# A fused attention and gated-FFN kernel: the first chunk's second product in row tiles, with its exchanged weights and two batches' loads moved to make that possible

## The chip, the cores and the metric

The kernel runs on one core of a Trainium2 chip. Times are device microseconds (us) of that core, as medians of several executions. A profile is one execution taken by the hardware profiler; its span is about 1.7 us shorter than the time of the same execution. The kernel before had the TensorE clock at full speed (granted clock 0.998 to 1.0).

## The reference

A causal attention with a forget gate (8 batches, 8 heads, 576 tokens, head size 64) whose output, as a matrix of 4608 tokens by 512, goes through a gated FFN with 1536 inner columns. Everything is given and returned in 32-bit floats.

```python
scores = (q @ k.T) / sqrt(64) + (cum[:, None] - cum[None, :])   # cum: cumulative log of f; causal mask
attn   = softmax(scores) @ v                                    # -> x, 4608 x 512
out    = (sigmoid(x @ w_gate) * (x @ w_val)) @ w_out            # 512 -> 1536 -> 512
```

## The kernel before

The FFN walks over nine chunks of 512 tokens. A chunk has 36 steps: 24 for the first product (x by w_gate and w_val), 12 for the second (by w_out). The attention of later batches is slipped in between these steps: score units (matmul, exp on ScalarE, causal mask on GpSimd) and, four heads at a time, an output *burst*, 120 small matmuls that make sums and values, after which VectorE scales x and SyncE exchanges the two halves of its partitions.

"Row tiles" means that in place of one matmul of 128 rows there are two of 64 rows, one on each half of the partitions. Such a pair took as long as one 128-row matmul: 10.36/48 = 0.216 us in the first profile (L495, 96 matmuls at 296.99 us), against 0.21 to 0.22 for L504. The first product and the second product of chunks 1 to 6 are in that form (`g2_twin`); chunks 0, 7 and 8 use full 128-row matmuls (`g2_full`). For the second half of its work the twin form, as written here, reads the operands with their partition halves exchanged: `gvx` (the activations, exchanged in each such chunk after column tiles 5, 9 and 11 of twelve) and `wox` (the output weights, exchanged once).

```python
    swap_bf = wox[:, NFT - 1, 0:128]
    xt = gvx[:, 0, :].rearrange("p (a d) -> p a d", d=64)
    # ...
    def cross_w2(x):                       # one piece of the exchanged weights, 2 tiles, 128 KB
        dst, src = ((LO, HI), (HI, LO))[x % 2]
        fs = slice(x // 2 * 2, x // 2 * 2 + 2)
        nc.sync.dma_start(wox[dst, fs, :], wo[src, fs, :])
    # ...
    TWIN = range(1, NTC - 2)

    def g1_end(c, ft):                     # end of one column tile of the first product
        # ... tanh on ScalarE, gate on VectorE -> gv[:, ft, :]
        if ft in (5, 9, 11) and c in TWIN:
            fs = slice({5: 0, 9: 6, 11: 10}[ft], ft + 1)
            nc.sync.dma_start(gvx[LO, fs, :], gv[HI, fs, 0:TCH // 2])
            nc.sync.dma_start(gvx[HI, fs, :], gv[LO, fs, TCH // 2:TCH])

    def g2_twin(c, y):
        x, qq, g = y // 6, y // 3 % 2, y % 3
        fb = 4 + 2 * qq
        n = TCH // 2
        for ft in range(4 * g, 4 * g + 4):
            for half, bk, o in ((LO, fb, 0), (HI, fb + 1, n)):
                if x == 0:
                    lhsT, rhs = gv[half, ft, o + qq * NP:o + (qq + 1) * NP], wo[half, ft, :]
                else:
                    lhsT, rhs = gvx[half, ft, qq * NP:(qq + 1) * NP], wox[half, ft, :]
                nc.tensor.matmul(ps[:, bk, :], lhsT, rhs, ...)
        # ... stores after the last piece

    def g2_full(c, x):
        tt, g = (x % 4, x // 4) if c == 0 else (x // 3, x % 3)
        for ft in range(4 * g, 4 * g + 4):
            nc.tensor.matmul(ps[:, 4 + tt, :], gv[:, ft, tt * NP:(tt + 1) * NP], wo[:, ft, :], ...)
    # ... the schedule: put(step, what)
    for x, w in enumerate((5, 9, 12)):
        put(w, lambda x=x: load_w2(x))
    for x, w in enumerate((18, 21, 22, 23)):            # queries and keys of batches 2 and 3
        put(w, lambda x=x: load_qk(2 + x // 2, x % 2, ((0, 4),)))
    for x in range(NFT):                                # exchanged weights, in chunk 1
        put(38 + 2 * x, lambda x=x: cross_w2(x))
```

The softmax here doesn't subtract the row's maximum and nothing guards it: scores larger than these inputs give would overflow.

## Time and profile before

| before | |
|---|---|
| time, median of 3 runs | 373.72 us (373.67 to 373.79) |
| span of the profiled run | 373.4 us, granted clock 0.998 |
| TensorE busy | 359.3 us, 96% of the span |
| first, second, third burst begin (a second profile of this kernel) | 45.79, 62.12, 87.01 us |

Two lines of the page matter for what follows: the DMA engines' busy share in 40 slices of the span (in tenths, 9.3 us a slice), which the prediction used only to ask when the exchanged data land, and the queue q8, of the kind "instruction", with packets, megabytes and its share of 16 engines' time, which it did not use.

```profile
DMA  8999999599988976789984996596313131011002
...
q8 instruction: 41, 0.67, 0.8%
```

In ten of the first eleven slices, about 100 us, the DMA engines are busy for 0.8 or more of the time. The second line looks negligible, 0.8%. I take it to be TensorE's own program, which the page does not say: 41 packets of 0.67/41 MB = 16 KB, for an engine with 5259 matmuls and 5264 weight loads in the trace, 10,523/41 = 257 a packet. From the first packet (15.23 us) to the last (358.47) the trace holds about 10,126 of them, 253 for each of 40 packets. So I estimate a packet at 256 instructions, a number that the places of the pauses bear out below.

### The profile page before, as it was taken

Reading aid. Unit: us, or ns where it says so; the run is one execution under the profiler, and the core shown is the slowest. Engines: PE = TensorE matmul, PEld = TensorE weight load, DVE = VectorE, ACT = ScalarE, POOL = GpSimd, SP = SyncE. Lnnn points to the kernel's source line nnn. Section 1 sums busy time; section 2 is a strip of 40 time slices with the busy share of each in tenths; the row PEclk is TensorE's granted clock in tenths of the full one; section 3 lists DMA queues with packets and bytes.
Section 4 is the critical chain, followed back from the end, with each engine's and each line's share of the span. In section 5 each row is a group of like instructions: output and inputs, shape, how many; then the busy total and the mean of one; then the engine's idle time right before and its main releaser. Section 6 shows DMA issues by size and latency. Waiting matters only on the chain.

```text
span 373.4 us, 12210 instructions
## 1 busy us (share of the span) xinstructions
PE 359.3 (96%) x5259; PEld 192.0 (51%) x5264; DVE 176.5 (47%) x382; ACT 195.7 (52%) x294; POOL 168.3 (45%) x265
## 2 busy tenths in 40 slices
PE   2889999999999999999999999999999999999996
PEld 1547545455555545454665566545456544444442
DVE  5775482557375555274708370737064703312320
ACT  5868754574736472848374727471747313323321
POOL 8896745064826663559665946460415000000000
PEclk9999999999999999999999999999999999999999
DMA  8999999599988976789984996596313131011002
GB/s 157 233 209 256 194 182 217 173 213 154 158 164 196 157 84 63 168 182 134 142 185 105 185 177 138 148 159 83 99 59 76 32 102 58 3 56 58 0 24 90
DMA packets 101350, 49.24 MB, mean 132 GB/s; under 512 B 72001, under 2 KB 94401, under 8 KB 101297
## 3 DMA queue, kind: packets, MB, share of 16 engines
q0 software_dynamic: 48704, 20.65, 44.0%
q1 hardware_dynamic: 52448, 27.68, 30.8%
q8 instruction: 41, 0.67, 0.8%
q10 hardware_dynamic: 144, 0.13, 0.1%
q14 instruction: 13, 0.10, 0.1%
HBM read 37.90 MB, written 9.44 MB: 127 GB/s over the span
## 4 chain that ended last, share of the span: by engine, by line
PE 94%; ACT 2%; DMA 1%; issue 1%; DVE 1%; POOL 0%; ACTq 0%; POOLq 0%
PE ps L455 51%; PE ps L495 17%; PE ps L352 8%; PE ps L504 8%; PE ps L241 6%; PE ps L195 2%; PE ps L300 1%; DMA qk_in<-in_k_dram 1%; ACT eC L246 1%; ACT eB L246 0%; ACT eA L246 0%; ACT kT L200 0%; PE ps L417 0%; DVE kT L200 0%; POOL qk_in L97 0%
## 5 line engine op out<-in xcount | busy, mean ns | idle before, releaser
L455 PE MATMUL ps<-xR,w 64*128 64x512 bf16 x1728 | 205.1, 376 | 0.2
L465 DVE SCALAR_TENSOR_TENSOR gv<-sg,ps 128x512 bf16<-128x512 bf16 x108 | 74.0, 686 | 152.2 <-ACT sg L464 149.0
L455 PEld LDWEIGHTS <-w 64*128 64x128 bf16 x1728 | 86.2, 94 | 84.0 <-issue 2.5
L464 ACT ACTIVATE sg<-ps 128x512 bf16<-128x512 f32 x108 | 64.5, 598 | 85.1 <-PE ps L455 83.9
L248 POOL TENSOR_SCALAR_AFFINE_SELECT eC<-eC 128x256 bf16<-128x256 bf16 x32 | 12.9, 404 | 94.4 <-ACT eC L246 94.4
L241 PE MATMUL ps<-qT,kT 64*128 64x320 bf16 (+6 forms) x416 | 47.0, 275 | 2.0 <-ACT kT L200 1.1
L246 ACT ACTIVATE eC<-ps 128x896 bf16<-128x896 f32 (+1 forms) x32 | 28.1, 878 | 20.7 <-PE ps L241 20.4
L257 POOL TENSOR_TENSOR vg<-vb,g_bf 128x640 bf16<-128x640 f32 x30 | 37.8, 1261 | 0.0
L482 ACT ACTIVATE ob<-ps 128x512 f32<-128x512 f32 x35 | 19.6, 596 | 32.2 <-PE ps L504 20.1
L495 PE MATMUL ps<-wox,gvx 64*128 64x512 bf16 x288 | 35.7, 376 | 0.0
L241 PEld LDWEIGHTS <-kT 64*128 64x128 bf16 x416 | 22.9, 96 | 24.0 <-issue 4.9
L246 ACT ACTIVATE eA<-ps 128x896 bf16<-128x896 f32 (+2 forms) x33 | 30.5, 926 | 9.0 <-PE ps L241 8.5
L495 PE MATMUL ps<-wo,gv 64*128 64x512 bf16 x288 | 34.4, 376 | 0.0
L246 ACT ACTIVATE eB<-ps 128x768 bf16<-128x768 f32 (+2 forms) x33 | 27.4, 832 | 10.0 <-PE ps L241 9.2
L504 PE MATMUL ps<-wo,gv 128*128 128x512 bf16 x140 | 32.1, 380 | 0.3 <-issue 0.2
L271 DVE TENSOR_TENSOR xR<-ps,R 128x64 bf16<-128x64 f32 (+2 forms) x68 | 26.2, 429 | 2.1
L108 POOL DMA_DIRECT2D vb<-in_v_dram x30 | 25.2, 849 | 0.2 <-issue 0.2
L263 DVE STREAM_TRANSPOSE R<-r 128x576 f32<-128x576 f32 (+1 forms) x32 | 24.6, 770 | 1.1
L495 PEld LDWEIGHTS <-gvx 64*128 64x128 bf16 x288 | 15.7, 94 | 13.0 <-issue 0.4
L495 PEld LDWEIGHTS <-gv 64*128 64x128 bf16 x288 | 15.3, 94 | 13.7 <-issue 0.5
L246 ACT ACTIVATE eD<-ps 128x640 bf16<-128x640 f32 x30 | 21.1, 702 | 2.0 <-PE ps L241 2.0
L504 PEld LDWEIGHTS <-gv 128*128 128x128 bf16 x144 | 13.4, 98 | 16.7 <-issue 1.4
(82 smaller groups left out, 325.9 us busy)
## 6 DMA issues: line engine op xcount, KB each, us to landing
out_dram<-ob SPq DMA_DIRECT2D x35, 256.0 KB, 2.2
vb<-in_v_dram POOLq DMA_DIRECT2D x20, 256.0 KB, 5.4
xR<-xR SPq DMA_DIRECT2D x20, 144.0 KB, 4.1
gvx<-gv SPq DMA_DIRECT2D x12, 192.0 KB, 4.8
vb<-in_v_dram SPq DMA_DIRECT2D x8, 256.0 KB, 7.3
k_rows<-in_k_dram POOLq DMA_DIRECT2D x16, 128.0 KB, 6.0
q_rows<-in_q_dram POOLq DMA_DIRECT2D x16, 128.0 KB, 5.6
qk_in<-in_q_dram POOLq DMA_DIRECT2D x7, 288.0 KB, 6.7
```

Of the source, the lines that this page charges most:

```text
L108: eng.dma_start(vbs[b % 2][0:n, t, h0:h1, :], rows)
L241: nc.tensor.matmul(ps[:, sc + h, c:c + i1 - i0], k_at(p, jt)[hp, :], qT[hp, i0:i1], start=True, stop=True)
L246: nc.scalar.activation(e[:, :, 0:w], ps[:, sc:sc + 2, 0:w], ACTF.Exp, scale=scale)
L257: (eng or nc.gpsimd).tensor_tensor(out=vg[:, :, :, 0:D], in0=vbs[b % 2][:, :, 2 * a:2 * a + 2, :], in1=g_bf[:, :, 2 * p:2 * p + 2].unsquee ...
L263: nc.vector.transpose(R.rearrange("p (n c) -> p n c", c=32), r.unsqueeze(2).to_broadcast([128, r.shape[1], 32]))
L271: nc.vector.tensor_tensor(out=xR[:, a, r0:r0 + n], in0=psf[:, o + i:o + i + n], in1=R[:, i:i + n], op=ALU.mult)
L352: nc.tensor.matmul(psf[32 * qd:32 * qd + 32, o + a:o + z], lhsT_of(jt, qd), e_of(u, qd)[:, c:c + z - a], start=(y == 0), stop=(y == len(to ...
L455: nc.tensor.matmul(ps[:, bk, :], w1[half, head, ft * NP:(ft + 1) * NP], xR[half, sl, t0:t0 + TCH], start=(first and x == 0), stop=(last an ...
L464: nc.scalar.activation(sg, ps[:, fb, :], ACTF.Tanh, scale=0.5)
L465: nc.vector.scalar_tensor_tensor(out=gv[:, ft, :], in0=sg, scalar=1.0, in1=ps[:, fb + 1, :], op0=ALU.add, op1=ALU.mult)
L495: nc.tensor.matmul(ps[:, bk, :], lhsT, rhs, start=(x == 0 and ft == 0), stop=(x == 1 and ft == NFT - 1))
L504: nc.tensor.matmul(ps[:, 4 + tt, :], gv[:, ft, tt * NP:(tt + 1) * NP], wo[:, ft, :], start=(ft == 0), stop=(ft == NFT - 1))
```

## The change

The intent: make the second product of chunk 0 a twin as well, so that TensorE no longer changes between the 128-row form and the 64-row form of the score units there (about 0.11 us a change, as the prediction reads it from 0.97 against 0.86 us in the trace). For that the exchanged weights are needed earlier, in chunk 0, and they are made in six large pieces instead of twelve small ones. To make room on the DMA queues, the queries and keys of batch 3 are loaded in chunk 1, and those of batch 2 one or two steps later in chunk 0. An interim value `xt` moves out of `gvx`, which chunk 0 now uses.

```diff
-    xt = gvx[:, 0, :].rearrange("p (a d) -> p a d", d=64)        # now in an output buffer
@@ cross_w2
-        fs = slice(x // 2 * 2, x // 2 * 2 + 2)
+        fs = slice(x // 2 * 4, x // 2 * 4 + 4)
@@ rest_values (rest_turn reads it again as st["xt"])
+        ob = osb.tile([128, DM], FP32, tag="ob", name="ob")
+        xt = st["xt"] = ob[:, 0:DM // 4].bitcast(BF16).rearrange("p (a d) -> p a d", d=64)
@@
-    TWIN = range(1, NTC - 2)
+    TWIN = range(0, NTC - 2)
@@ g2_full
-        tt, g = (x % 4, x // 4) if c == 0 else (x // 3, x % 3)
+        tt, g = divmod(x, 3)
@@ schedule
-    for x, w in enumerate((18, 21, 22, 23)):
+    for x, w in enumerate((20, 22, 50, 54)):
         put(w, lambda x=x: load_qk(2 + x // 2, x % 2, ((0, 4),)))
-    for x in range(NFT):
-        put(38 + 2 * x, lambda x=x: cross_w2(x))
+    for x in range(6):
+        put((19, 21, 23)[x // 2], lambda x=x: cross_w2(x))
```

More of the change, by code (lines that the diff above doesn't have):

```diff
@@ L430, in rest_turn @@
         slot_free(1)
+        xt = st["xt"]
         halves = ((LO, 3), (HI, 2))
```

## The prediction

> **What bounds the kernel now.** I read the page first. TensorE is busy 359.3 of 373.4 us at full clock and the chain that ended last is 94% TensorE, so only what TensorE itself does, or waits for, sets the time. In the chain in order of time I then looked at chunk 0's second product (steps 24 to 35, line L504, one 128-row matmul per weight tile) and at the same stage of later chunks (L495, two 64-row matmuls side by side). Columns are start, length, engine and line, count.
>
> ```profile
> PE 359.3 (96%) x5259; PEld 192.0 (51%) x5264; DVE 176.5 (47%) x382; ACT 195.7 (52%) x294; POOL 168.3 (45%) x265
> PE 94%; ACT 2%; DMA 1%; issue 1%; DVE 1%; POOL 0%; ACTq 0%; POOLq 0%
> ...
> 296.99 10.36 PE ps L495 x96
> ```
>
> The last line is a whole second product in row tiles without anything between: 96 matmuls, 48 pairs, 10.36/48 = 0.216 us a pair. A 128-row matmul of L504 also takes 0.216 us (5.13 us for 23 records of 24, the trace having lost one: 5.13/24 = 0.214). So row tiles make no matmul faster; what can be won lies in the changes between forms. For that I read the timeline of TensorE, where starts can be compared: first chunk 0's second product with its score units (L241), then score units of the same shapes inside a first product (L455, row tiles already).
>
> ```profile
> 57.17 1.04 PE L504 MATMUL ps<-wo,gv 128*128 128x512 bf16 x4
> 58.14 0.36 PE L241 MATMUL ps<-qT,kT 64*128 64x448 bf16 x2
> 58.43 1.04 PE L504 MATMUL ps<-wo,gv 128*128 128x512 bf16 x4
> 59.40 0.53 PE L241 MATMUL ps<-qT,kT 64*128 64x256 bf16 x8
> 59.87 1.04 PE L504 MATMUL ps<-wo,gv 128*128 128x512 bf16 x4
> ...
> 80.98 0.35 PE L241 MATMUL ps<-qT,kT 64*128 64x448 bf16 x2
> 81.17 1.03 PE L455 MATMUL ps<-xR,w 64*128 64x512 bf16 x8
> 82.03 0.36 PE L241 MATMUL ps<-qT,kT 64*128 64x256 bf16 x4
> 82.23 1.03 PE L455 MATMUL ps<-xR,w 64*128 64x512 bf16 x8
> ```
>
> A group of four L504 matmuls holds TensorE from 57.17 to 58.14, 0.97 us; eight L455 ones hold it 82.03-81.17 = 0.86. The 448-column unit holds it 0.29 beside L504 and 0.19 beside L455. So each change between the 128-row and the 64-row form costs about 0.11 us, in each direction.
>
> Last, the engines that feed the output burst (L352) in the middle of this stage, from the timelines of ScalarE and GpSimd:
>
> ```profile
> 61.31 0.71 ACT L246 ACTIVATE eD<-ps 128x640 bf16<-128x640 f32 x1
> ...
> 59.91 1.26 POOL L257 TENSOR_TENSOR vg<-vb,g_bf 128x640 bf16<-128x640 f32 x1
> 61.13 0.63 POOL L248 TENSOR_SCALAR_AFFINE_SELECT eA<-eA 128x512 bf16<-128x512 bf16 x1
> 61.72 0.28 POOL L248 TENSOR_SCALAR_AFFINE_SELECT eB<-eB 64x128 bf16<-64x128 bf16 x1
> 62.09 0.41 POOL L248 TENSOR_SCALAR_AFFINE_SELECT eD<-eD 128x256 bf16<-128x256 bf16 x1
> ...
> 62.47 0.37 PE L352 MATMUL ps<-eD,g_bf 128*32 128x256 bf16 x4
> ```
>
> The burst starts at 62.08, just as ScalarE is done with eD (61.31+0.71 = 62.02), and its eD matmuls stand at 62.47 with 0.37 us, where the first burst's take 0.28: they wait for the mask of eD on GpSimd (62.09+0.41 = 62.50). So at this place ScalarE, GpSimd and TensorE are level. That decides how much of the saving survives.
>
> [...] The trace shows their mean busy share over 0.9 in most of the first 65 us and 0.24 in 65 to 70 us, so I take it that what is added before 65 us competes with loads.
>
> **The change part by part.**
> (a) Second product of chunk 0: out go 48 full matmuls (48 x 0.216 = 10.37 us), in come 48 pairs (10.36). Nothing. Twice the weight loads, 94 ns each, two in 216 ns: hidden, as in the later chunks.
> (b) Changes of form. Score units stand at four places between the quads: four changes out of the 128-row form, 4 x 0.105 = 0.42 us, and four back (B+D 0.41 for 0.29; C 0.29 for 0.19; A+B 0.47 for 0.36; D 0.24 for 0.13) = 0.44. Into the burst: the last quad held 62.08-61.08 = 1.00, estimated 0.95 in row tiles: 0.05. Out of it: last L352 start 64.24 to first L504 64.62 is 0.38; in chunk 1 from 103.78 to the first L495 at 103.93 is 0.15: 0.23. Transposes (64x64) are another form in both versions: no difference. Sum 0.42+0.44+0.05+0.23 = 1.14 us of TensorE.
> (c) What the other engines let through. From the first score unit (0.1 earlier) ScalarE runs eB, eD, eC without a pause in the kernel before, so eC's exp ends at 59.36 for 59.46, and GpSimd then runs the mask of eC, the value scaling, the masks of eA, eB, without a pause: all only 0.1 earlier. The mask of eB ends at 61.90, and that of eD, which no longer waits for ScalarE (its last exp gains the 0.35 us pause before eA and ends near 61.6), runs from about 61.88 to 62.29. TensorE would be at the burst by about 61.5, waits for ScalarE's eD until about 61.65, and its eD matmuls for GpSimd until 62.3. Against 62.50 that saves 0.2, not the 0.9 that TensorE had gained by there. After the burst the 0.23 of (b) comes in full. Sum 0.2+0.23 = about 0.45 us.
> (d) Exchanged weights, 12 transfers of 128 KB in chunk 1 become 6 of 256 KB in chunk 0. In SyncE's order they stand behind earlier pieces: the first pair goes once the first third of the output weights has landed (issued 33.97, landing some 8 to 9 us: about 43), the second behind gv of tile 9 (51.0), the third behind the exchange of the first burst's x (54.5 to 55.8), so issued by 57.0, then the last gvx pair by 58.3. Such a piece of 128 KB landed in 3.5 to 6.1 us, a last gvx in about 4; estimated here: all landed by about 63. The crossed half starts after the burst, near 64, and needs the last third near 66. Some 2 us to spare.
> (e) Value loads of batch 2 now stand behind these, issued from 58.3 instead of 55.85; they took 8.56 us to issue, landed by 67.8, and are wanted by the scaling at 74.1: still hidden.
> (f) Queries and keys of batch 3: four transfers leave 47 to 57 us and go to steps 50 and 54 (about 84 to 91 us), wanted at step 67 (106.6); they landed in 6 to 7.2 us. GpSimd pays the same 0.65 us each, behind the masks that the burst of step 52 needs. Hidden both times; it does relieve the queue exactly where (d) loads it.
> (g) The interim copy xt moves from gvx to an output buffer, free at that time: no cost. Outputs of chunk 0 are evicted two at step 32 and two at step 35 instead of one in each; the second pair needs about 1.3 us on ScalarE, and its banks are wanted 0.41+0.97+0.41 = 1.8 us later: no wait.
>
> **The rivals.**
> 1. The whole 1.14 us comes through (time 372.6): if GpSimd's chain in front of the burst is looser than I read. For it: the profile marks only short waits there. Against it: the eD matmuls of 0.37 us.
> 2. Late data (374 to 375): the crossed half at step 30 or 32 waits for wox or gvx. For it: the DMA engines are over 0.9 busy up to 65 us, and one value load needed 4.2 us on SyncE; landings beyond 8 us occur. Against it: 2 us to spare and four competing loads gone. A variant is the second burst's x exchange, issued at 68.8, wanted by chunk 1's first tiles at about 72.9, landing in 3.7: almost no room, so a value load still in the queue then would cost half a microsecond.
> 3. Nothing at all (373.7): the pauses of TensorE called "issue" (0.43 us at 127.6, 0.30 at 254.3) stand at no place that the program explains; 96 more matmuls and loads shift them, and may cost or give 0.3 us.
>
> **Range and chances.** 373.72 - 0.45 = 373.27, written as 373.2 as rival 1 is likelier than 2. The range reaches from the full saving, 372.6, to 373.8, where a small wait eats it. 2% is 7.5 us, more than the whole stage's overhead: faster 0.005, same 0.985, slower 0.01.
>
> **What would show it.** Right: no L504 in chunk 0, quads of 0.86 us from start to start, score units of 0.13 to 0.29; from the first second-product matmul (54.93) to the first transpose of step 36 about 14.3 us instead of 14.75; a wait of TensorE for ScalarE and GpSimd at the burst of 0.3 to 0.8 us; exchanged weights landed by 63 us; from there on all shifted evenly. Wrong: a burst that starts by 61.5 without waits (rival 1), or a gap in front of the first crossed matmuls or in steps 36 to 39 with a DMA as its releaser (rival 2).

What is cut at its mark are rules quoted from outside. The sum is 0.42+0.44+0.05+0.23 = 1.14 us of TensorE, of which 0.2 and 0.23, written as about 0.45, were to come through. In the sentence left there, "their" means the 16 DMA engines.

## The result, and the profile after

| | before | after |
|---|---|---|
| time, median of 4 runs of the same rounds | 373.75 us (373.67 to 374.22) | 377.41 us (377.21 to 378.25) |
| span of the profiled run | 373.4 us; 372.0 in two later profiles | 375.7 us |

The ratio is 1.0099, with a 95% interval of 1.0082 to 1.0117. Ratios here are the mean time of one kernel's runs over that of the other's of the same rounds, so not quite the ratio of the medians. Executions over 1.5% slower than the fastest of the same kernel are left out of the means. The kernel became 3.7 us slower where 0.5 us faster was forecast.

The changed kernel's page, busy times and the chain's shares by engine:

```profile
PE 359.3 (96%) x5309; PEld 188.4 (50%) x5312; DVE 176.6 (47%) x382; ACT 195.3 (52%) x294; POOL 168.5 (45%) x265
...
PE 90%; ACT 3%; DMA 3%; DVE 2%; issue 2%; POOL 0%; SPq 0%; DVEq 0%; ACTq 0%; POOLq 0%
```

TensorE is as busy as before, 359.3 us. All that was lost is waiting: TensorE's share of the chain fell from 94 to 90%, that of DMA rose from 1 to 3% and that of "issue" from 1 to 2%.

The first profile of the kernel before happened to hold three "issue" pauses (0.13, 0.43 and 0.30 us in its chain, near 48.5, 127.6 and 254.3 us) and a span of 373.4; a second and a third profile of the same kernel had spans of 372.0 us with none of them, or with one alone (0.40 us near 253). I compare with the second. Its chain, in order of time (start, length, engine and line, count; L352 is a burst, L455 the first product, L504 the full second product):

```profile
45.79 2.21 PE ps L352 x120
48.00 2.70 PE ps L455 x24
...
54.99 1.83 PE ps L504 x8
...
62.12 2.34 PE ps L352 x102
64.46 5.29 PE ps L504 x24
69.74 0.41 PE ps L195 x36
```

And the chain of the changed kernel (burst L351, first product L457, twin L497, the exchange of x issued at L280):

```profile
45.65 2.21 PE ps L351 x120
47.85 0.97 PE ps L457 x7
48.82 1.21 issue
50.03 2.11 PE ps L457 x17
...
56.41 1.83 PE ps L497 x16
...
63.09 1.11 PE ps L351 x34
...
70.57 4.46 DMA xR<-xR
75.03 0.04 issue
75.07 0.61 PE ps L457 x4
...
216.97 0.60 PE ps L351 x42
217.57 1.03 issue
218.61 0.21 PE ps L351 x3
```

Three things are new. TensorE pauses at 48.8 us, in the first product, with nothing there to wait for: its 24 matmuls take 0.97+1.21+2.11 = 4.29 us instead of 2.70. (The ends of matmuls in the trace are modelled, so the 1.59 us between these sums say more of a pause than the 1.21 written beside it.) From 70.57 a transfer stands on the path, the exchange of the second burst's x, 4.46 us long. And at 217.6 us, far from anything that was changed, a burst is cut three matmuls from the end of a group.

Because most of TensorE's work did not change, the clearest ledger is the distance from one burst's start to the next one's:

| stretch | before (us) | after (us) | difference | what lies in it |
|---|---|---|---|---|
| start to 1st burst | 45.79 | 45.65 | -0.14 | loads |
| 1st to 2nd | 16.33 | 17.44 | +1.11 | early pause, row tiles |
| 2nd to 3rd | 24.89 | 26.02 | +1.13 | wait for x, burst |
| 3rd to 4th | 14.75 | 14.96 | +0.21 | moved queries and keys |
| 8th to 9th | 17.57 | 17.89 | +0.32 | pause near 185 us |
| 10th to 11th | 21.21 | 22.27 | +1.06 | pause at 217.6 us |
| sum of these | | | +3.69 | spans: 375.7 - 372.0 = 3.7 |

All other stretches are equal within 0.02 us. So the loss is whole in these rows.

**What the pauses are.** Counting the matmuls and weight loads in the trace up to each pause (`--windows` from 0) gives 1469 for the one at 48.8 us and 7097 for the one at 217.6; in the first profile of before, 4283 for its pause at 127.6 us and 8117 for that at 254.3. Divided by 256 they leave 189, 185, 187 and 181: every pause stands at the same place within a block of 256 instructions, but for the few that the count leaves out. I take it to be the end of a 16 KB packet of program, so that TensorE waits there for its own instructions. That is inferred, from these remainders and from the 257 instructions a packet; queue q8 shows when the packets came. Queues of the changed kernel from 47 to 48 us (packets, MB, share of 16 engines):

```profile
q0 software_dynamic: 134, 0.13, 75.8%
...
q8 instruction: 1, 0.02, 5.9%
```

and of the kernel before from 46 to 47 us:

```profile
q0 software_dynamic: 129, 0.12, 74.3%
q8 instruction: 1, 0.02, 5.6%
```

Each of these packets takes about 0.9 us of a DMA engine's time (5.9% of 16 us). In narrower windows the packet of the changed kernel begins at 47.4 us and TensorE goes on at 50.03; in the kernel before (this profile) it begins at 46.2 and there is no pause. Over ten traces, here and below, with a pause near 48 us the pause ends 2.3 to 2.6 us after the packet begins. How long it is follows from when the packet begins, counted from the moment at which TensorE enters the block before: of the fourteen traces without idle instructions, 0.7 to 1.7 us later in the nine with no pause there or one of up to 0.33 us, 2.2 to 3.4 in the five with a pause of 1.1 to 2.2 us; in the kernel before 1.0 (45.20 to 46.20 us; 1.2 in its first profile, 44.92 to 46.13), in the changed kernel 2.2 (45.27 to 47.46). A block that holds a burst is short: its 240 instructions took 2.21 us, and this whole block of the changed kernel 3.55 (45.27 to 48.82). The packet began within it, 2.2 us after its start, and TensorE went on 2.57 us after that (47.46 to 50.03), so there was no time to spare: against the kernel before it began 1.0 to 1.2 us later after the block's start, and the pause is 1.21 us instead of none or 0.13. What delays it in the changed kernel must be found among the transfers near it.

### The profile page after: what moved, and what is told of

Read it like the earlier page. It is cut to its first block, busy times and chain, and to the rows that moved or that the text cites. A ratio compares the mean times of both kernels' runs of the same rounds, so it can differ in the third digit from the quotient of the medians.

```text
span 375.7 us, 12313 instructions
## 1 busy us (share of the span) xinstructions
PE 359.3 (96%) x5309; PEld 188.4 (50%) x5312; DVE 176.6 (47%) x382; ACT 195.3 (52%) x294; POOL 168.5 (45%) x265
## 4 chain that ended last, share of the span: by engine, by line
PE 90%; ACT 3%; DMA 3%; DVE 2%; issue 2%; POOL 0%; SPq 0%; DVEq 0%; ACTq 0%; POOLq 0%
PE ps L457 50%; PE ps L497 17%; PE ps L351 8%; PE ps L240 6%; PE ps L506 6%; PE ps L194 2%; DMA qk_in<-in_k_dram 1%; PE ps L299 1%; DMA xR<-xR 1%; ACT eB L245 1%; ACT eC L245 1%; DVE xR L270 1%; ACT eA L245 1%; DVE R L262 0%; ACT eD L245 0%
## 5 line engine op out<-in xcount | busy, mean ns | idle before, releaser
L457 PE MATMUL ps<-xR,w 64*128 64x512 bf16 x1728 | 205.5, 376 | 2.2 <-issue 1.2
L457 PEld LDWEIGHTS <-w 64*128 64x128 bf16 x1728 | 85.9, 94 | 87.1 <-issue 5.2
L497 PE MATMUL ps<-wox,gvx 64*128 64x512 bf16 x336 | 40.7, 376 | 0.0
L497 PE MATMUL ps<-wo,gv 64*128 64x512 bf16 x336 | 40.5, 376 | 0.0
L497 PEld LDWEIGHTS <-gvx 64*128 64x128 bf16 x336 | 16.4, 94 | 17.0
L497 PEld LDWEIGHTS <-gv 64*128 64x128 bf16 x336 | 16.4, 94 | 16.8 <-issue 0.7
L247 POOL TENSOR_SCALAR_AFFINE_SELECT eA<-eA 128x512 bf16<-128x512 bf16 (+2 forms) x33 | 20.5, 622 | 4.4 <-ACT eA L245 4.2
L351 PEld LDWEIGHTS <-vg 128*32 128x32 bf16 x1120 | 19.9, 97 | 2.5 <-issue 1.1
```

The lines of the kernel that those rows point to most:

```text
L247: nc.gpsimd.affine_select(out=m, in_=m, compare_op=ALU.is_ge, fill=0.0, base=0, pattern=pat, channel_multiplier=-1)
L351: nc.tensor.matmul(psf[32 * qd:32 * qd + 32, o + a:o + z], lhsT_of(jt, qd), e_of(u, qd)[:, c:c + z - a], start=(y == 0), stop=(y == len(to ...
L457: nc.tensor.matmul(ps[:, bk, :], w1[half, head, ft * NP:(ft + 1) * NP], xR[half, sl, t0:t0 + TCH], start=(first and x == 0), stop=(last an ...
L497: nc.tensor.matmul(ps[:, bk, :], lhsT, rhs, start=(x == 0 and ft == 0), stop=(x == 1 and ft == NFT - 1))
```

## The experiments

Each group of runs was made on one chip with runs of the kernel before between them; ratios are against these. I give the median, the ratio with its interval and the distances from burst to burst that matter, in the order 1-2, 2-3, 3-4, 10-11. The kernel before has 16.33, 24.89, 14.75, 21.21. Pauses are those of one profiled execution, which is not always a typical one.

### First group: one part of the change at a time

**The kernel before, unchanged**, one look.

> The kernel before, unchanged, for a second trace. Its profiled run of the first trace took 375.15 us where its other runs take 373.7, so that trace holds some 1.4 us that is not usual. If TensorE's pauses called issue (0.13 us at 48.5, 0.43 at 127.6, 0.30 at 254.3) belong to places of the program, they stand in the same places again with the same lengths. If they are chance, they move or go, and the span is nearer 372.0 than 373.4 us.

373.74 us, span 372.0. This is the profile used above. The pauses of the first profile at 127.6 and 254.3 us are gone: pauses come and go between executions of the same kernel.

**Only the early exchange of the weights.**

```diff
-        fs = slice(x // 2 * 2, x // 2 * 2 + 2)
+        fs = slice(x // 2 * 4, x // 2 * 4 + 4)
-    for x in range(NFT):
-        put(38 + 2 * x, lambda x=x: cross_w2(x))
+    for x in range(6):
+        put((19, 21, 23)[x // 2], lambda x=x: cross_w2(x))
```

> The kernel before with only the weight exchange moved into chunk 0 (six pieces of 256 KB at steps 19, 21 and 23); chunk 0's product stays 128 rows deep, nothing in chunk 0 needs the exchanged weights. Theory 1, transfers: the loss of 3.7 us is made by the moved exchange, which holds up TensorE's instruction supply at 48.8 us (1.2 us) and the x exchange at 74 us (0.8 us): time 375 to 378 us and both gaps are there. Theory 2, form: the loss comes with the row tiles of chunk 0: time 373.4 to 374.0 us and neither gap.

376.40 us against 374.36, 1.0059 (1.0028 to 1.0090). Distances 17.79, 24.89, 14.76, 21.21: of these four only the first has grown. A pause of 1.11 us stands at 48.74, and the instruction packet begins at 47.2. The early weights alone, with nothing that reads them, bring the early pause. The wait for x, which theory 1 expected too, did not come.

**The early exchange and the moved loads, without the row tiles.**

```diff
 w2_early, and
-    for x, w in enumerate((18, 21, 22, 23)):
+    for x, w in enumerate((20, 22, 50, 54)):
```

> The changed kernel without the row tiles: weight exchange in chunk 0 and batch 3's queries and keys in chunk 1, chunk 0's product as before. Against the changed kernel (377.4 us) it has only the row tiles and the interim copy less. Theory 1: 377 to 378 us, as the row tiles themselves gain 0.3 us by the two traces. Theory 2: 373.4 to 374.0 us.

375.24 us, 1.0025 (1.0001 to 1.0049). Distances 16.97, 24.89, 14.96, 21.21; a pause of 0.29 us at 48.32 and one of 0.55 at 253.61. With fewer queries and keys in the queues the packet begins at 46.2, and little of the early pause is left. The third distance has grown by 0.21. The time met neither theory.

**Only the moved loads**, the same last edit on the kernel before.

> The kernel before with only batch 3's queries and keys moved from chunk 0 to steps 50 and 54. Both theories: within 0.3 us of the kernel before (373.7 us), and the x exchange of the second burst, with less in the queue, no later than before. A loss of over 1 us would be a third theory: loads in chunk 1 delay the masks or the instruction supply there.

376.38 us (375.44 to 379.69), 1.0079 (1.0024 to 1.0133): I had expected no more than 0.3 us. Distances 16.30, 24.89, 14.95. The profiled execution has pauses of 0.90 us at 107.2 and 0.46 at 128.1, none early. The 0.20 us of the third distance is steady; the rest of the loss differs much from run to run, as the range of 4 us shows (the run of 379.69 us had a granted clock of 0.994).

### Second group: shifting the block boundaries

If the later pauses and the late x come from where the 256-instruction blocks begin, they must move when idle instructions are put in. 80 idle transposes of 64x64, put at the very start where TensorE waits for the first loads, are 160 instructions (a weight load and a matmul each); with the 96 that the change adds, 256, so all later boundaries fall where they fell before.

**The changed kernel again.**

> The changed kernel, unchanged, on the chip of this group. Supply theory (TensorE's instructions come in 16 KB packets of 256 instructions each through one DMA engine; where such a packet is late, TensorE pauses some 1.6 to 1.7 us after the packet's end): the packets stand at the same instructions again, so pauses stand again at about 48.8 us (1 us) and 217.6 us (1 us), and the x exchange wait at 74 us is there if the packet near 71.9 us again falls into the exchange. Time 3 to 4 us over the kernel before. Chance theory: pauses at other places.

378.38 us against 375.11, 1.0086 (1.0056 to 1.0116). The chain of this execution:

```profile
48.44 0.97 PE ps L457 x7
49.40 2.19 issue
51.59 3.80 PE ps L457 x17
```

The early pause is at the same matmul but 2.19 us long, and the packet began at 49.2. The 17 matmuls behind it took 3.80 us instead of 2.11, because TensorE had lost half its clock. This is the view by stretches, for the pause and for what follows it (bounds, length, busy time of TensorE, its weight loads, VectorE, ScalarE and GpSimd, then granted clock, DMA share and GB/s):

```profile
49.40:51.59 2.19, 0.00 (x1) 0.00 (x0) 1.40 (x2) 0.00 (x0) 0.00 (x0) 1.00 1.11 220
51.72:55.13 3.41, 3.41 (x17) 1.08 (x13) 1.01 (x3) 0.60 (x1) 0.00 (x0) 0.50 1.19 203
```

So this pause cost 2.19 us and then 1.7 more at half clock. The same window of 3.41 us follows the longest stops in two other traces (below), and none follows a pause of up to 1.99 us; what sets it off three traces do not settle. In the timed runs it shows as a mean clock of 0.994 or 0.995: four of the six runs here have it and took 378.3 to 379.1 us, the two at full clock 376.2 and 376.3. The medians of this group have to be read with that. The x exchange landed in 2.5 us this time, and there was no wait for it; at 219.7 us stands a pause of 0.56. So the same boundaries cost different amounts in different executions.

**The first pair of exchanged weights one step later.**

```diff
-        put((19, 21, 23)[x // 2], lambda x=x: cross_w2(x))
+        put((20, 21, 23)[x // 2], lambda x=x: cross_w2(x))
```

> The changed kernel with the first pair of weight exchange pieces one step later (step 20), which puts it behind the gvx pieces of tile 9 in SyncE's order, so it is issued at about 52 us instead of 45.2. Supply theory: the packet of about 47.4 us then comes at 46.2 as in the kernel before, the pause at 48.8 us shrinks from 1.21 us to 0.3 us or less, all else is as in the changed kernel: about 1 us faster than it. Rival (the pause comes from the number of instructions or from chance): no change of that pause. Risk for both: with 1 MB of exchange from 52 us on, the crossed half at 65 us may wait for it.

376.81 us, 1.0057 (1.0031 to 1.0084). The median is lower than the changed kernel's by more than the 1 us expected, but only because all six runs kept the clock: against the two full-clock runs above nothing was gained. In the mechanism it is a miss: the early pause stayed, 1.99 us at 48.21. The trace shows why: the exchanged activations of tiles 0 to 5, issued at about 39 us, are what moves between 42 and 48 us, and the weights are only issued behind them. To take the early pause away, both have to go.

**The changed kernel with 160 idle instructions.**

```diff
+    for _ in range(80):
+        nc.tensor.transpose(psh[LO, 6144:6208], ident_bf[LO, LO], ident_bf[LO, LO])
```

> The changed kernel with 80 idle 64x64 transposes (160 instructions) ahead of the first, in the time in which TensorE waits for queries. From chunk 1 on, each instruction then stands at the same place within its packet of 256 as in the kernel before (96 + 160 = 256). Supply theory: the packet of 71.9 us moves to about 73 us, the x exchange wait at 74 us (0.8 us) goes, and the pause of 1.0 us at 217.6 us goes (instead perhaps those of the kernel before at 127 and 254 us, 0.3 to 0.5 us); the packet of 47.4 us moves too, so the pause at 48.8 changes. Time 1 to 2.5 us under the changed kernel. Rival: transposes that change nothing leave all pauses where they are, time equal or up to 0.5 us longer.

377.47 us, 1.0078 (1.0051 to 1.0104). Distances 17.60, 25.04, 14.95, 21.22: the wait for x and the pause at 217 us are gone, as expected. But the early pause is not, it only moved with its boundary:

```profile
52.33 0.37 PE ps L194 x31
52.70 1.53 issue
54.23 0.25 PE ps L194 x5
```

The time gained nothing that can be shown: 0.9 us against the median of the changed kernel of the same rounds, with intervals that overlap, and that median holds four runs with the half-clock window, this one a single one.

**The kernel before with 96 idle instructions**, 48 such transposes.

> The kernel before with 48 idle 64x64 transposes (96 instructions) ahead of the first: from chunk 1 on each instruction stands within its packet as in the changed kernel, with no other part of the change. Supply theory: a packet falls into the second burst's x exchange near 71 us, with up to 0.8 us of wait at 73 us, and a pause of about 1 us appears at about 215 us: 1 to 2 us slower than the kernel before. Rival: equal to the kernel before within 0.3 us.

375.84 us, 1.0030 (1.0009 to 1.0051). Distances 16.33, 25.47, 14.76, 22.94. Its chain:

```profile
70.43 4.04 DMA xR<-xR
...
214.84 2.29 PE ps L352 x99
217.13 1.71 issue
218.84 0.21 PE ps L352 x3
```

Nothing of the change is in this kernel but its count of instructions, and it has the slow x exchange (4.04 us) and the pause at 217 us, with the same three matmuls left. The stretch in which the changed kernel pauses near 185 us is longer too, by 0.6 us. That is the clearest single run, with one caution: the profiled execution, 377.67 us, is the slowest of seven, the others took 375.5 to 376.2. On average the 96 idle instructions cost 0.3%, about 1.1 us. Most boundaries are crossed without a pause: the first profile of the kernel before has 41 packets and three pauses. Where a pause did stand, of 0.13 to 2.78 us over all runs, a burst lay in the block or just before it in most cases, as here.

Why x comes late is seen in the queues of the changed kernel from 71 to 72 us:

```profile
q1 hardware_dynamic: 170, 0.18, 77.2%
q8 instruction: 1, 0.02, 11.4%
```

A packet of program, 11.4% x 16 = 1.8 us long here, falls into the middle of the exchange; between 73.3 and 74.6 us only single small packets are left in flight, and the exchange lands in 4.46 us. In the kernel before no such packet lies in it and it lands in 2.5. That the packet makes the transfer late is shown by moving it (4.04 us with the 96 idle instructions, 2.4 with the 160), and the trace shows how: the program packet ends at 73.75 us, and from 73.74 on the last eight pieces of the exchange (1152 bytes each, one sixteenth of its 128) start one after the other. In all five traces with a slow exchange (3.6 to 4.5 us) exactly eight pieces start so at the packet's end; the packet had begun 2.0 to 2.1 us after the exchange was issued. Where no packet begins until 2.7 us after the issue, the exchange lands in 2.4 to 3.3 us.

### Third group: the row tiles without their transfers, and the transfers late

**The row tiles alone.** The crossed half reads `gv` and `wo` instead of `gvx` and `wox`, so no transfer is moved. The result is wrong (relative error 0.33).

```diff
-    TWIN = range(1, NTC - 2)
+    TWIN = range(0, NTC - 2)
-        if ft in (5, 9, 11) and c in TWIN:
+        if ft in (5, 9, 11) and c in TWIN and c:
-                if x == 0:
+                if x == 0 or c == 0:
```

> Wrong result on purpose: chunk 0's product in row tiles, but its crossed half reads the plain gv and the plain weights, so that no transfer of the kernel before moves or is added (the exchange stays in chunk 1). It holds the row tiles and their 96 more TensorE instructions alone. Supply theory: chunk 0's stage is 0.3 to 0.45 us shorter; the pause near 48.5 us is as in the kernel before (0 to 0.5 us, not over 1); but the packets of chunk 1 on stand as in the changed kernel, so one lies in the second burst's x exchange near 71 us (wait 0.5 to 0.9 us) and a pause of 1 to 1.8 us stands near 216 us. Time 1 to 2 us over the kernel before. Rival (only the moved transfers cost): 0.3 to 0.5 us under the kernel before, neither the wait nor the pause.

375.35 us against 374.48, 1.0019 (0.9997 to 1.0040): less than expected and not clear of the noise, so the traces have to decide. Distances 16.39, 26.01, 14.76, 22.71. The early pause is 0.15 us and the third distance is that of before. The slow x exchange (4.4 us) and a pause of 1.47 us at 215.6 are there, as in the kernel with nothing but 96 idle instructions.

**The same with 160 idle instructions** (wrong).

> The run before with 160 idle instructions at the start, so that packets from chunk 1 on stand as in the kernel before. Supply theory: neither the wait near 73 us nor the pause near 216 us, instead at most 0.5 us near 127 and 254 us; an early packet moves to about 43 and 51 us, where the untouched loads may or may not hold it up. Time 0.5 us under to 0.5 us over the kernel before.

377.20 us, 1.0066 (1.0046 to 1.0085). Distances 16.73, 26.21, 14.76, 21.22. A miss in time: the later pauses went, but the boundaries now fall at 52.73 us (0.65) and at 66.66, into the second burst (0.97 us). The padding was put ahead of the first boundary of concern, so it shifted good places too.

**Nothing exchanged before 51 us.**

```diff
-        if ft in (5, 9, 11) and c in TWIN:
-            fs = slice({5: 0, 9: 6, 11: 10}[ft], ft + 1)
+        if ft in ((5, 9, 11) if c else (9, 11)) and c in TWIN:
+            fs = slice({5: 0, 9: 6 if c else 0, 11: 10}[ft], ft + 1)
-        put((19, 21, 23)[x // 2], lambda x=x: cross_w2(x))
+        put((20, 21, 23)[x // 2], lambda x=x: cross_w2(x))
```

> The changed kernel with nothing exchanged before 51 us: the gvx pieces of tiles 0 to 5 go with those of tiles 6 to 9, the first pair of weight pieces at step 20. In the run with only the weights moved to step 20 the packet still came at 47.5 us, behind the gvx pieces of tiles 0 to 5, which moved from 42 to 48 us. Supply theory: without them it comes at about 46 us as in the kernel before and the pause at 48.5 us falls from 1.2 to 2.2 us to 0.5 us or less; the wait at 74 us and the pause at 217 us stay. Time 1 to 1.5 us under the changed kernel, 1.5 to 2.5 over the kernel before. If the crossed half waits for data at 63 to 66 us instead, the gain is lost there.

375.56 us, 1.0024 (1.0008 to 1.0040). The loss is about 1 us, under the 1.5 to 2.5 expected. The result is right, and no matmul waits for the exchanged data. Distances 16.57, 25.12, 14.97, 22.69. The early pause fell to

```profile
47.70 0.33 issue
48.03 2.11 PE ps L457 x17
```

with the packet at 45.6 us instead of 47.4. So the exchange transfers at 42 to 48 us are the cause of the early pause. The wait for x, which I had expected to stay, was absent here (landing 2.5 us): the program packet came 2.7 us after the exchange was issued, when it was all but done; the pauses at 182.6 (0.39) and 215.1 us (1.46) stayed.

**The same with 160 idle instructions.**

> The run before with the 160 idle instructions: the wait at 74 us and the pause at 217 us should go too, as they did with the same padding of the changed kernel, while a packet at about 51.5 us meets the exchanges that now all start at 51 us: a pause of 1 to 1.5 us near 52.7 us is expected there. Time equal to the kernel before up to 1.5 us over it.

379.07 us, 1.0112 (1.0085 to 1.0139). Distances 15.97, 29.71, 14.97, 21.22. A miss: no pause stands near 52.7 us, and the time is 4.6 us over the kernel before. A boundary in the second burst brings the longest pause, and a window at half clock (68.10 to 71.51 us) follows it, so that the second distance of 29.71 us holds both:

```profile
62.65 2.49 PE ps L351 x101
65.14 2.78 issue
67.92 0.20 PE ps L351
```

The first distance, in which this run has no pause, is what the row tiles are worth by themselves: 15.97 against 16.33, 0.36 us less. It is one trace; the last run below, the only other one in row tiles without an early pause, has 0.17 less.

### Fourth group: can a version win?

**The kernel before against itself.**

> The kernel before against itself, for the noise: ratio 1.000 within 0.2%. If its trace has pauses, they stand near 48.5, 127.6 or 254 us and nowhere else, each 0 to 0.6 us.

374.06 against 373.98 us, 1.0001 (0.9986 to 1.0016), span 372.0, one pause of 0.40 us at 252.8. So differences of 0.2% can be told apart.

**The changed kernel with chunk 2 in full matmuls**, which takes the 96 instructions out again after 141 us.

```diff
-    TWIN = range(0, NTC - 2)
+    TWIN = (0, 1, 3, 4, 5, 6)
```

> The changed kernel with chunk 2's second product in 128-row form, which takes the 96 instructions out again at about 140 us, and touches nothing at the start. Supply theory: the early pause (1 to 2.2 us near 48.8) and the x exchange wait (0.8 us near 74) stay, the pauses near 185 and 217 us (0.3 and 0.6 to 1.8 us) go, in exchange for the changes of form in chunk 2 (about 0.3 us) and perhaps 0.3 us near 254: 0.8 to 1.5 us under the changed kernel. Rival (the pause at 217 comes from anything else of the change): it stays, and the time is 0.3 us over the changed kernel.

378.52 us (376.63 to 380.54), 1.0120 (1.0088 to 1.0153). Distances 17.95, 25.20, 14.95, 21.21: the pauses near 185 and 217 us are gone, as expected. But the 128-row form costs 1.28 us in chunk 2 (36.28 us for a chunk of 35.0, 0.2 of it a wait for an output store), where I had expected 0.3. And three of the six runs have a clock of 0.995 (379.5 to 380.5 us; the others 376.6 to 377.5). So the time missed.

**The late exchange with chunk 2 in full matmuls.**

> The run without any exchange before 51 us, plus chunk 2 in 128-row form. That run was 1.0 us over the kernel before, with 0.33 us of pause at 47.7, 0.39 at 182.6 and 1.46 at 215.1. Supply theory: the last two go for 0.3 us of changes of form: 0.3 to 0.7 us under the kernel before. Rival: no change, 1 us over it.

376.17 us, 1.0055 (1.0036 to 1.0074). Distances 16.48, 25.04, 14.95, 21.23; early pause 0.25. All large pauses are gone and 1.28 us are paid in chunk 2. It was to beat the kernel before and does not. The profiled execution, 374.96 us, is the fastest of six; what the others lost besides no trace shows.

**And with the queries and keys of batch 3 early again.**

```diff
-    for x, w in enumerate((20, 22, 50, 54)):
+    for x, w in enumerate((18, 21, 22, 23)):
```

> The run before with batch 3's queries and keys loaded in chunk 0 as in the kernel before. Every trace with these loads at steps 50 and 54 spent 14.95 us between two bursts of chunk 1 where the others spent 14.75. Without contention it should be 0.2 us faster than the run before; but the loads then meet the exchanges between 51 and 60 us, and if the crossed half or a packet is late for it, it is 0.5 to 1.5 us slower.

382.75 us, 1.0240 (1.0212 to 1.0267). The third distance is 14.75 again, but the crossed half has to wait for its data, and the half clock follows: all six runs have a clock of 0.991 to 0.996, the profiled one a window from 70.04 to 73.45 us. Its chain:

```profile
51.02 10.11 DMA gvx<-gv
61.12 0.02 issue
61.14 9.30 DMA wox<-wo
70.44 0.04 issue
70.48 5.07 PE ps L497 x31
```

With these loads moved the same kernel took 376.17 us, so their move is what makes room for the exchange. No version tried is faster than the kernel before.

## Why the prediction was wrong

**The TensorE terms, (a) and (b): right, but for one.** The prediction's quads of 0.86 us and units of 0.13 to 0.29 us are there. The timeline of TensorE in the changed kernel (start, length, what):

```profile
59.37 0.36 PE L240 MATMUL ps<-qT,kT 64*128 64x448 bf16 x2
59.55 1.04 PE L497 MATMUL ps<-wo,gv 64*128 64x512 bf16 x8
60.42 0.70 PE L240 MATMUL ps<-qT,kT 64*128 64x256 bf16 x8
...
```

The unit holds TensorE 59.55-59.37 = 0.18 us instead of 0.29, the quad 60.42-59.55 = 0.87 instead of 0.97 (the quad ahead of these still takes 0.98). From the first second-product matmul to the burst the time fell from 62.12-54.99 = 7.13 to 63.09-56.41 = 6.68, by 0.45. The exit term of 0.23 us did not exist: it came from the first start seen after the burst, and the trace of before had lost a matmul just there. In the second profile the chain has 24 full matmuls directly behind the burst, at 64.46, without a gap.

**The other engines, (c): roughly right.** The mask of eD stands at

```profile
63.23 0.40 POOL L247 TENSOR_SCALAR_AFFINE_SELECT eD<-eD 128x256 bf16<-128x256 bf16 x1
```

on GpSimd, 6.88 us after the twin's first matmul (56.35) instead of 7.16: 0.28 earlier, where 0.2 was forecast. The burst begins earlier but then waits for masks, 2.49 us instead of 2.34 in runs without other trouble. Together: -0.36 in the first distance (-0.17 in the other trace), +0.15 in the second (25.04 against 24.89), at most about 0.2 us gained, where 0.45 was forecast.

**The moved loads, (f): wrong by 0.20 us.** "Hidden both times" fails: from the third to the fourth burst 14.95 to 14.97 us in every trace with these loads at steps 50 and 54, and 14.75 or 14.76 in every other. This alone takes back what the row tiles gained. What exactly the loads hold up there I did not settle.

**The exchange, (d): the step that failed.** The prediction asked only whether the exchanged data come in time. They do, though with less room than the 2 us forecast: the last pieces were issued at 57.7 to 59.9 us and landed 6.0 to 6.7 us later, at about 65 to 66 us instead of 63, and the crossed half began at 65.5. No matmul of the changed kernel waits for `gvx` or `wox`, and even with everything after 51 us none does. What it did not ask is what these transfers do to others. They move on the same 16 DMA engines as the packets of q8 (from 47 to 48 us q1, which carries the exchanges, had 41.8% of these 16, q8 5.9%), and the packet that TensorE, as I read it, needs right after the first burst begins at 47.4 us instead of 46.2. That costs 1.59 us in the changed kernel (4.29-2.70), and in another execution a pause of 2.19 us and 1.7 us more at half clock. The early weights alone bring it (pause 1.11), the row tiles without the transfers do not (0.15), and holding the transfers back takes most of it away (0.33).

**Rival 3, the pauses, was right in kind and too small.** It said that 96 more instructions shift the pauses and "may cost or give 0.3 us". It took them as pauses that "stand at no place that the program explains". They do stand at such a place, 181 to 189 instructions into a counted block of 256, and one in a burst or up to 3 us behind it cost up to 2.8 us where it showed. In the changed kernel 0.32 and 1.06 us of the ledger are this.

**Rival 2 was right in place, wrong in cause.** Its variant, the second burst's x exchange with "almost no room", is the second largest loss of the ledger, 1.13 us less the 0.15 of the burst, about 1.0, sized at half a microsecond. Its "landing in 3.7" is a misreading: that is the first burst's exchange, the second burst's landed in 2.5 in the second profile. The cause was not a value load in the queue but the packet of program, shifted by 96 instructions: 96 idle instructions alone bring 4.04 us of landing and 0.58 of loss (25.47-24.89). Its main form, late exchanged data, is real only when batch 3's loads stay early (379.1 us of span).

**The sum.** Row tiles about -0.2, moved loads +0.2, early pause about +1.5, x about +1.0, later pauses 0.32+1.06; with -0.14 at the start that makes 3.7, the measured difference of the spans. The last two come with 96 idle instructions alone, the early pause with the early exchange alone; no row tile is needed for any of the three, only a different timing of TensorE's program against the data transfers. The range, 372.6 to 373.8, had nothing of that size in it.

**What stays open.** That q8 carries TensorE's program is inferred from counts and times. That a program packet is late because it stands behind queued data in a DMA engine is inferred from start times, not seen packet by packet; only the reverse, an x exchange behind a program packet, is seen so. The early pause of 1.2 us in one execution and 2.2 in another goes with a packet that began 2.2 and 3.4 us after TensorE had entered the block before; why that differed I did not find. And single profiles tell where a pause was, not how often it comes. The ledger explains one execution; the timed runs do not add up from parts (the early weights cost 2.0 us and the moved loads 2.0 in the medians, both together 0.9).

## What to carry to other kernels

In this kernel, 96% one engine, the "issue" pauses were read by counting that engine's instructions. The four counted ones stood at 181 to 189 within a block of 256, and near 48 us they ended 2.3 to 2.6 us after a packet of q8 began, from which I take it that the engine waited for its own program. The places to protect were the bursts (240 instructions in 2.21 us) while the DMA queues are full: in the second burst one pause was 2.78 us. A transfer that arrives in time itself can still cost by what it delays: the early weights alone, which nothing read, brought a pause of 1.11 us. A change of the instruction count shifted the later fetches: 96 idle instructions alone brought a pause of 1.71 us near 217 us. So it should be tested by itself with idle instructions before a loss far from the change is explained by the change's logic. A gain of half a microsecond on paper is below what such shifts did here (about 1 to 3 us), so a forecast of it needs a range of that width. And before executions are compared, look at the granted clock of each: here one window at half clock cost 1.7 us in a trace, and the runs of the changed kernel that had it took about 2 us longer than those without.
